# Spreading one zero fill over the DMA engines: six uneven transfers become 28 small ones and a nested tail

## The chip, the cores and the metric

The kernel runs on one core of a Trainium2 chip. The metric is the time of one execution on the device, in microseconds; lower is better. A core has the compute engines TensorE (PE in the profile), VectorE (DVE), ScalarE (ACT) and GpSimd (POOL), SyncE (SP), which here only issues transfers and waits, and 16 DMA engines that move the data.

## The reference

The reference is a decode step of a small transformer block together with its backward pass. Its inputs are one token of width 448, a K cache and a V cache of 8 heads x 32768 positions x 256, and the weights, all bfloat16. Only the last 4096 positions of the caches are read.

```python
h  = x + attention(layernorm(x), K[:, :, -4096:], V[:, :, -4096:], wq, wo)   # 16 query heads, 8 K/V heads
h2 = h + ((layernorm(h) @ w_gate) * (layernorm(h) @ w_up)) @ w_down
out, vjp = jax.vjp(forward, x, K, V, wq, wo, w_gate, w_up, w_down)
return out, *vjp(grad_out)
```

The gradients of K and V have the full shape of the caches, 8 x 32768 x 256 each (134 MB). Only their last 4096 positions of each head are computed; the other 28672 are zero and have to be written all the same. These zeros are most of the bytes that the kernel moves.

## The kernel before, in words

The work has four stages. The first goes over the eight K/V heads `g`: it loads K and V of the window (2 MB each, `load_kv`), computes the scores and the softmax (`scores`) and the sums that the backward pass needs (`moments`). The second does the output projection, the second layernorm and the gated layer, forward and backward. The third (`dq_all`) makes the gradient of the queries. The fourth goes over the heads again, makes the gradients of K and V for the window, and stores them from ScalarE's queue (`LD`, L739, 16 stores of 2 MB), while GpSimd makes the weights' gradients and stores them from its own queue.

Beside all this run the zero fills. There are 16 regions (8 heads, K and V), each of 28672 x 256 elements, 14 MB. The first two (`EARLY`) are written from the tile `pair`, the other 14 by `fill_late` from the tile `home` (`Z_late`), of whose rows every fourth partition, 0, 4, ..., 124, is kept at zero (`clear_rows`). A row is 8192 elements (`ZW`), 16 KB; a region is 896 rows, and a fill is one transfer, 32 partitions x `NZ` = 28 copies. SyncE (`ZQ`) issues the fills one after another: fill `i` waits until fill `i-2` has landed (`DEEP` = 2 semaphores, `zsem`), so that two are under way at any time. All transfers are issued by `fill_with` (L244), whose semaphore goes up by 16 when a transfer has landed. At the end `fills_done` lets VectorE wait for all fills (`psem` for GpSimd's transfers, `zsem` for SyncE's) and write `done_t` (L287).

One fill, that of region 3 (`UNEVEN`, the second of `fill_late`), is not written as one transfer. 22 x 32 of its rows are; the other 192 are written by six transfers of `e` source partitions x `rows` copies each, four from GpSimd's queue (3x8, 2x2, 3x13, 8x13) and two from SyncE's (4x5, 1x1), all ahead of the fill's main part.

The order on each engine is that of the program: `tc.keep_in_program_order` holds the fills and their waits in place, and they are set aside from the scheduler's own dependences. GpSimd's four transfers stand behind its loads of V for heads 5 and 6 (L207) and ahead of its load of the second half of the last K (L418).

Of the kernel before, what the change touches and what calls it, by code (L numbers as in the profile page):

```python
# [27 lines left out]
ZW = 16 * KB  # L28
# [7 lines left out]
def kernel(  # L36
        ctx, tc, A_x, A_k_cache, A_v_cache, A_wq, A_wo, B_x, B_w_gate, B_w_up, B_w_down, grad_out,
           out_0, out_1, out_2, out_3, out_4, out_5, out_6, out_7, out_8):
    nc = tc.nc
    LD = nc.scalar  # L40
    ZQ = nc.sync
# [29 lines left out]
    Z_late = home[:]  # L71
# [134 lines left out]
    def load_kv(dst, cache, g, queue=LD):  # L206
        queue.dma_start(out=dst, in_=cache[0, g, Sk - W:, :].rearrange("(p t) d -> p t d", t=T))  # L207
# [32 lines left out]
    def rows_of(src, n):  # L240
        return src[0:128:4].unsqueeze(1).to_broadcast([32, n, src.shape[1]])

    def fill_with(dst, src, sem, group, queue=ZQ):
        fill = queue.dma_start(out=dst, in_=src)  # L244
        tc.info.no_tile_sem_insts.add(fill.ins.name)
        tc.add_to_no_dep_group(group, fill.ins)
        tc.keep_in_program_order(fill.then_inc(sem, 16))
# [7 lines left out]
    for g in (5, 6):  # L255
        load_kv(V_of[g], A_v_cache, g, nc.gpsimd)

    def fill_late():
        zsem = [tc.alloc_semaphore(f"zsem{j}") for j in range(DEEP)]
        psem = tc.alloc_semaphore("psem")  # L260
        due = [0] * DEEP
        for i, reg in enumerate(regions[EARLY:]):
            j = i % DEEP
            if i >= DEEP:
                tc.keep_in_program_order(ZQ.wait_ge(zsem[j], due[j]))
            n = NZ
            if i + EARLY == UNEVEN:
                odd = reg.rearrange("(r f) -> r f", f=ZW)[22 * 32:]
                reg = reg[0:22 * 32 * ZW]
                n = 22  # L270
                at = 0
                for e, base, rows, queue in ((3, 0, 8, nc.gpsimd), (2, 12, 2, nc.gpsimd), (3, 20, 13, nc.gpsimd), (8, 64, 13, nc.gpsimd), (4, 0, 5, ZQ), (1, 0, 1, ZQ)):
                    fill_with(odd[at:at + e * rows].rearrange("(e n) f -> e n f", e=e),
                              Z_late[base:base + 4 * e:4].unsqueeze(1).to_broadcast([e, rows, ZW]), zsem[j] if queue is ZQ else psem, "fills", queue)
                    at += e * rows
                    if queue is ZQ:
                        due[j] += 16
            for dst, src in [(reg.rearrange("(p n f) -> p n f", p=32, f=ZW), rows_of(Z_late, n))]:
                fill_with(dst, src, zsem[j], "fills")
                due[j] += 16  # L280
        return zsem, psem, due

    def fills_done(zsem, psem, due):
        tc.keep_in_program_order(nc.vector.wait_ge(psem, 64))
        for j in range(DEEP):
            tc.keep_in_program_order(nc.vector.wait_ge(zsem[j], due[j]))
        filled = tc.keep_in_program_order(nc.vector.memset(done_t[:], 0.0))  # L287
        tc.declare_fence(filled.ins, group="fills")
# [43 lines left out]
    with tc.tile_pool(name="ps_x", bufs=1, space=bass.MemoryType.PSUM) as ps_x, \  # L332
# [72 lines left out]
        for g in range(G):  # L405
            p_f = p_next
            if g < G - 2:
                p_next = scores(g + 1)
            if g == 1:
                clear_rows()  # L410
                fill_sems = fill_late()
            moments(g, p_f)
            for w, h in NEXT.get(g, ()):
                load_kv((K_of, V_of)[w][h], (A_k_cache, A_v_cache)[w], h)
            if g == G - 4:
                LD.dma_start(out=K_of[G - 1][:, 0:T // 2, :], in_=k_last[:, 0:T // 2, :])
            if g == G - 2:
                nc.gpsimd.dma_start(out=K_of[G - 1][:, T // 2:, :], in_=k_last[:, T // 2:, :])  # L418
                p_next = scores(G - 1)
                LD.dma_start(out=wo_sb[:, JW:], in_=wo_v[:, JW:])  # L420
                LD.dma_start(out=dh_bc[0:1, :], in_=A_x.rearrange("a b d -> (a b) d"))
# [179 lines left out]
    with tc.tile_pool(name="work2", bufs=2) as work2, tc.tile_pool(name="lnw", bufs=1) as lnw, \  # L601
# [94 lines left out]
        for it, g in enumerate((6, 1, 3, 4, 5, 0, 7, 2)):  # L696
# [52 lines left out]
            if it == 6:  # L749
# [16 lines left out]
                nc.vector.tensor_copy(out=dx_bf[:, 384:D], in_=dx_ps[0:1, 384:D])  # L766
                LD.dma_start(out=out_1.rearrange("a b d -> (a b) d"), in_=dx_bf)
        fills_done(*fill_sems)

# [28 lines left out]
```

## Time and profile before

| what | value |
|---|---|
| median of 3 runs | 779.52 us (779.39 to 779.62) |
| the profiled execution | 779.39 us; span 777.6 us |
| granted clock of TensorE, mean | 0.74 |
| bytes moved | 330.40 MB, 425 GB/s over the span |
| HBM read, written | 49.38 MB, 280.59 MB |
| packets of SyncE's queue, ScalarE's, GpSimd's | 14826, 4266, 4272 |
| last store of a computed gradient issued | 747.9 us of the span |
| last fill issued by SyncE | 661.7 us of the span |

The span runs from the first to the last instruction; the execution's own time is 1.8 us longer. In the profile, the 40 digits of a row show how busy an engine was in each fortieth of the span, in tenths. The row DMA is the mean over the 16 DMA engines. The queue of a transfer is named by the engine that issues it: q1 is SyncE's, q10 ScalarE's and q0 GpSimd's. All three use the same 16 DMA engines. "x" behind a group is its count; a name such as `out_dram<-home` gives what is written and from what.

### The profile page before, as it was taken

The numbers are of one execution on the slowest core, as the hardware profiler recorded it, in microseconds if no ns is written. First come the engines' busy times: TensorE is split into PE (matmuls) and PEld (weight loads), VectorE is DVE, ScalarE is ACT, GpSimd is POOL, SyncE is SP. The second block draws the span as 40 slices with busy tenths as digits, with TensorE's granted clock in tenths as the row PEclk, the third lists the DMA queues.
The fourth block names the chain that finished last, engine by engine and source line by source line (L and its number), as shares of the span: only waits on it lengthen the run. The fifth ranks groups of instructions, "written<-read, shape, count | busy, mean of one in ns | idle before, by whom it ended". The sixth has DMA issues, their size and how long they took to land.

```text
span 777.6 us, 6520 instructions
## 1 busy us (share of the span) xinstructions
PE 450.8 (58%) x2205; PEld 191.2 (25%) x2205; DVE 382.6 (49%) x1132; ACT 198.6 (26%) x309; POOL 196.5 (25%) x113
## 2 busy tenths in 40 slices
PE   1999999796993755231142898532108886830310
PEld 1444444342441322010021233210003332300100
DVE  8168656351570723332369428463104853679520
ACT  1442332334200100000001127332103733540220
POOL 7000001000000010020001157363293938196000
PEclk9999999898896776555555799755558965765555
DMA  9999999999999999999999999999999999999997
GB/s 378 429 422 423 433 438 417 429 429 427 429 430 430 429 430 429 431 431 428 429 432 432 430 429 430 431 429 431 432 432 429 429 429 430 431 429 428 432 431 300
DMA packets 23398, 330.40 MB, mean 425 GB/s; under 512 B 1920, under 2 KB 2181, under 8 KB 4645
## 3 DMA queue, kind: packets, MB, share of 16 engines
q1 hardware_dynamic: 14826, 250.43, 75.4%
q10 hardware_dynamic: 4266, 53.39, 16.1%
q0 software_dynamic: 4272, 26.17, 8.0%
q8 instruction: 17, 0.28, 0.1%
q14 instruction: 17, 0.13, 0.0%
HBM read 49.38 MB, written 280.59 MB: 424 GB/s over the span
## 4 chain that ended last, share of the span: by engine, by line
DVE 16%; PE 15%; DMA 14%; another core or an unknown queue 4%; ACT 2%; issue 1%; DVEq 0%; ACTq 0%
DMA out_dram<-arena 11%; PE d_ps L729 4%; PE rows_ps L322 4%; DVE pair L753 3%; PE tr_ps L319 3%; DVE arena L737 3%; DVE arena L736 3%; DVE arena L551 2%; PE dqb_ps L607 2%; DVE arena L704 1%; DMA arena<-in_B_w_up_dram 1%; PE dqb_ps L613 1%; DMA arena<-in_A_v_cache_dram 1%; ACT arena L734 1%
## 5 line engine op out<-in xcount | busy, mean ns | idle before, releaser
L381 DVE TENSOR_SCALAR arena<-arena,p_f 128x256 bf16<-128x256 bf16 x512 | 109.4, 281 | 29.9 <-PE M_t L385 29.9
L319 PE MATMUL tr_ps<-ident_f,arena 128*128 128x128 f32 x448 | 83.0, 316 | 63.1 <-DMA arena<-in_A_v_cache_dram 41.0
L322 PE MATMUL rows_ps<-arena,vpad 128*16 128x512 bf16 x256 | 87.8, 437 | 11.8 <-DVE arena L704 5.9
L338 ACT COPY arena<-tr_ps 128x1024 bf16<-128x1024 bf16 x64 | 63.5, 1013 | 109.0 <-PE tr_ps L319 105.0
L319 PEld LDWEIGHTS tr_ps<-ident_f,arena 128*128 128x128 f32 x448 | 55.3, 157 | 109.8 <-issue 60.5
L729 PE MATMUL d_ps<-arena 32*128 32x512 bf16 x256 | 48.3, 519 | 55.1 <-DVE arena L737 45.1
L385 PE MATMUL M_t<-arena 128*128 128x512 bf16 x320 | 78.7, 392 | 0.0
L736 DVE CAST arena<-d_ps 128x512 bf16<-128x512 f32 x64 | 44.1, 688 | 49.6 <-PE d_ps L729 48.9
L737 DVE CAST arena<-d_ps 128x512 bf16<-128x512 f32 x64 | 43.5, 680 | 20.9 <-DMA out_dram<-arena 20.9
L733 ACT CAST arena<-d_ps 128x512 bf16<-128x512 f32 x64 | 37.8, 590 | 62.0 <-PE d_ps L729 60.2
L702 ACT COPY arena<-tr_ps 128x1024 bf16<-128x1024 bf16 x32 | 32.6, 1020 | 76.2 <-PE tr_ps L319 57.1
L734 ACT CAST arena<-d_ps 128x512 bf16<-128x512 f32 x64 | 38.2, 596 | 20.5 <-DMA out_dram<-arena 20.5
L385 PEld LDWEIGHTS <-arena 128*128 128x128 bf16 x320 | 30.5, 101 | 38.5 <-issue 10.1
L505 PE MATMUL r_ps<-arena,X2pad 128*2 128x448 bf16 x24 | 10.3, 564 | 49.5 <-DMA arena<-in_B_w_gate_dram 39.1
L324 DVE COPY rows_t<-rows_ps 16x512 f32<-16x512 f32 x8 | 5.4, 679 | 63.4 <-PE rows_ps L322 63.3
L729 PEld LDWEIGHTS <-arena 32*128 32x128 bf16 x256 | 11.1, 96 | 94.1 <-DVE arena L737 60.2
L624 POOL TENSOR_SCALAR arena<-dh_bc,oX_f 128x448 bf16<-128x448 bf16 x18 | 25.1, 1402 | 27.9 <-DMA out_dram<-arena 27.8
L207 POOL DMA_DIRECT2D pair<-in_A_v_cache_dram x2 | 1.3, 632 | 114.7 <-POOLq L253 114.7
L436 POOL DMA_DIRECT2D arena<-in_B_w_gate_dram x4 | 3.1, 773 | 105.9 <-DVE dhn L495 64.5
L704 DVE COPY arena<-tr_ps 128x1024 bf16<-128x1024 bf16 x32 | 22.5, 704 | 14.7 <-PE tr_ps L319 13.4
L322 PEld LDWEIGHTS <-vpad 128*16 128x16 bf16 x256 | 17.4, 90 | 45.0 <-issue 41.0
L385 PE MATMUL M_t<-arena,pair 128*128 128x512 bf16 x128 | 28.0, 379 | 0.0
(257 smaller groups left out, 641.3 us busy)
## 6 DMA issues: line engine op xcount, KB each, us to landing
out_dram<-home SPq DMA_DIRECT2D x13, 14336.0 KB, 78.9
out_dram<-arena ACTq DMA_DIRECT2D x16, 2048.0 KB, 18.6
out_dram<-pair SPq DMA_DIRECT2D x2, 14336.0 KB, 93.6
out_dram<-home SPq DMA_DIRECT2D x1, 11264.0 KB
arena<-in_A_k_cache_dram ACTq DMA_DIRECT2D x4, 2048.0 KB, 20.7
arena<-in_A_k_cache_dram SPq DMA_DIRECT2D x3, 2048.0 KB, 19.6
arena<-in_A_v_cache_dram SPq DMA_DIRECT2D x3, 2048.0 KB
arena<-in_A_v_cache_dram ACTq DMA_DIRECT2D x3, 2048.0 KB, 32.8
```

The source lines that it names most:

```text
L319: nc.tensor.transpose(tr_ps[:, i, :], X_sb[:, 4 * q + i, :].bitcast(f32), ident_f[:])
L322: nc.tensor.matmul(rows_ps[:], lhsT=pad[:, e, 16 * q:16 * q + 16], rhs=XT.rearrange("p (n e) -> p n e", e=2)[:, :, e], start=(q == 0 and e ...
L338: sT_ps = dots(K_of[g], KT_slot, vpad[g % 2], rows1, ps_c, "cols", lambda q, XT, ps: nc.scalar.copy(out=XT, in_=ps))
L381: nc.vector.tensor_scalar(out=pK[:, i, hh, :], in0=K_sb[:, t, :], scalar1=p_f[:, 8 * i + c, hh:hh + 1], scalar2=None, op0=ALU.mult)
L385: nc.tensor.matmul(M_ps[vh], lhsT=V_sb[:, t, vh * 128:(vh + 1) * 128], rhs=pK[:, i, :, :].rearrange("p h d -> p (h d)"), start=(t == 0), s ...
L702: nc.scalar.copy(out=XT, in_=ps)
L704: nc.vector.tensor_copy(out=XT, in_=ps)
L729: nc.tensor.matmul(d_ps[:, qi].rearrange("p w d -> p (w d)"), lhsT=rm[32 * q:32 * (q + 1), l, :], rhs=Rs[32 * q:32 * (q + 1), :], start=Tr ...
L733: nc.scalar.copy(out=stV[:, t:t + 2, :], in_=d_ps[:, :, 0, :])
L734: nc.scalar.copy(out=stK[:, t:t + 2, :], in_=d_ps[:, :, 1, :])
L736: nc.vector.tensor_copy(out=stV[:, t:t + 2, :], in_=d_ps[:, :, 0, :])
L737: nc.vector.tensor_copy(out=stK[:, t:t + 2, :], in_=d_ps[:, :, 1, :])
```

## The change

The uneven fill is spread in another way. Its main part falls from 22 copies of each of the 32 partitions to 14, 448 rows. The other 448 rows go in two sets. GpSimd issues 28 transfers ahead of the main part, in 14 pairs: for `m` from 1 to 14, one of `m` partitions x 1 row and one of `16 - m` partitions x 2 rows. SyncE issues 14 transfers behind the last fill of all, of 14 partitions x 1 row, then 13, and so on down to 1, with no wait between them; they count on the semaphore of the last fill, and the last wait on it grows with them. A new helper, `fill_rows`, writes `k` partitions (0, 8, 16, ... from `8 * e0`) x `n` rows. `psem` is waited for at 28 x 16 instead of 64. The number of bytes is the same, and nothing else is changed.

```diff
+    def fill_rows(rows, at, e0, k, n, sem, queue):
+        fill_with(rows[at:at + k * n].rearrange("(e n) f -> e n f", e=k),
+                  Z_late[8 * e0:8 * (e0 + k):8].unsqueeze(1).to_broadcast([k, n, ZW]), sem, "fills", queue)
+
...
             n = NZ
             if i + EARLY == UNEVEN:
-                odd = reg.rearrange("(r f) -> r f", f=ZW)[22 * 32:]
-                reg = reg[0:22 * 32 * ZW]
-                n = 22
+                n = 14
+                single = reg.rearrange("(r f) -> r f", f=ZW)[n * 32:]
+                reg = reg[0:n * 32 * ZW]
                 at = 0
-                for e, base, rows, queue in ((3, 0, 8, nc.gpsimd), (2, 12, 2, nc.gpsimd), (3, 20, 13, nc.gpsimd), (8, 64, 13, nc.gpsimd), (4, 0, 5, ZQ), (1, 0, 1, ZQ)):
-                    fill_with(odd[at:at + e * rows].rearrange("(e n) f -> e n f", e=e),
-                              Z_late[base:base + 4 * e:4].unsqueeze(1).to_broadcast([e, rows, ZW]), zsem[j] if queue is ZQ else psem, "fills", queue)
-                    at += e * rows
-                    if queue is ZQ:
-                        due[j] += 16
+                for m in range(1, 15):
+                    for e0, k, rows in ((0, m, 1), (m, 16 - m, 2)):
+                        fill_rows(single, at, e0, k, rows, psem, nc.gpsimd)
+                        at += k * rows
             for dst, src in [(reg.rearrange("(p n f) -> p n f", p=32, f=ZW), rows_of(Z_late, n))]:
                 fill_with(dst, src, zsem[j], "fills")
                 due[j] += 16
+        for k in range(14, 0, -1):
+            fill_rows(single, at, 0, k, 1, zsem[j], ZQ)
+            due[j] += 16
+            at += k
         return zsem, psem, due
 
     def fills_done(zsem, psem, due):
-        tc.keep_in_program_order(nc.vector.wait_ge(psem, 64))
+        tc.keep_in_program_order(nc.vector.wait_ge(psem, 28 * 16))
```

In the program as built, the very first of GpSimd's transfers, one partition x one row, is written as 16 pieces of 512 elements; every other one keeps its rows of 8192 elements.

## The prediction

> **What bounds the kernel now.** I read the page first, its slices and queues.
>
> ```profile
> span 777.6 us, 6520 instructions
> PE 450.8 (58%) x2205; PEld 191.2 (25%) x2205; DVE 382.6 (49%) x1132; ACT 198.6 (26%) x309; POOL 196.5 (25%) x113
> ...
> DMA  9999999999999999999999999999999999999997
> ...
> q1 hardware_dynamic: 14826, 250.43, 75.4%
> q10 hardware_dynamic: 4266, 53.39, 16.1%
> q0 software_dynamic: 4272, 26.17, 8.0%
> ```
>
> No compute engine is busy for more than 58%, while the 16 DMA engines are full in every slice but the last; the queue shares add up to 99.6% of their span. q1 is SyncE's queue, q10 ScalarE's, q0 GpSimd's. So the bytes set the time, and the open question is how evenly the 16 engines finish. Next, the timeline and the stretches of the end:
>
> ```profile
> 746.36 1.55 ACTq L739 DMA_DIRECT2D out_dram<-arena  x2
> 776.50 0.06 DVE L287 MEMSET done_t<- 1x1 f32 x1 [29.61 <-DMA out_dram<-home]
> 700.00:747.00 47.00, 8.61 (x48) 3.06 (x48) 35.77 (x41) 9.32 (x17) 13.14 (x3) 0.50 1.01 431
> 747.00:762.00 15.00, 0.00 (x0) 0.00 (x0) 0.00 (x0) 0.00 (x0) 0.00 (x0) 0.50 1.01 433
> ```
>
> After 747.9 us no compute is left; VectorE waits 29.61 us for the fills, and all engines stay full until past 762. Compute has about 19 us of room: from 747 on an engine moves 47 rows (28.9 us at 0.61), of which the last two stores are 16, 9.8 us. Last, the DMA slices of 765 to 777.6 us alone:
>
> ```profile
> DMA  7979798969698969686747221321101010000000
> q1 hardware_dynamic: 126, 1.80, 33.4%
> ```
>
> The share falls from 9 to 0 over some 7 us: the engines run dry one after another, and the last sets the end.
>
> **Which engine is last.** The trace has each DMA packet's queue, start, duration and bytes, but no engine. It can be worked out: a packet starts 3 or 4 ns before the one ahead of it on its engine ends, and each engine must follow the order of rows of each queue. I strung all packets into 16 chains so. A 16 KB row takes 0.611 us, so 0.607 net. The chains show where the uneven fill's 192 rows go: GpSimd's four transfers lie on engines 0-2 (8 rows each), 3-4 (2), 5-7 (13) and 8-15 (13), next to one another; SyncE's on 0-3 (5 each) and on 0 (1). An engine with no part in a GpSimd transfer gets a 4-byte packet per row instead: 13x8 + 14x2 + 13x13 + 8x13 = 405, just what q0 has beyond its 37x16 completions. I number the engines by these places. Sums: engine 0 has 14 rows, 1 and 2 have 13, 3 has 7, 4 has 2, the rest 13. The ends, us of the span:
>
> ```
> engine 0: 770.4; 1 and 2: 770.9, 771.5; 3: 774.1; 4: 775.9
> engines 5-15: 769.2 769.4 769.6 772.1 772.2 772.2 772.4 772.4 772.4 772.6 774.4
> ```
>
> Mean 772.0. So engine 4, with the fewest rows, is still last. Its packets run over: between 42 and 748 us most of its rows take 3 to 60 ns (a few up to 140) too long, 13.4 us in all, where most engines lose 1 to 2. (Engines 4 to 15 have equal histories after the uneven fill, so chains can change places where two end together; I read the overrun, which leaves one chain and begins in another at 315.8 and at 550.0 us, as one engine.) Engine 3 carries most of the 8 KB packets of q14, 0.31 us each and some 0.35 more for the row behind.
>
> **The change part by part.** The uneven fill's plain part falls from 44 rows an engine to 28: -16 on all. The 14 nested SyncE transfers put 14 rows on engine 0 down to 1 on 13, none on 14 and 15 (before: 4 rows wide on engines 0-3, 1 wide on 0; lowest first). So engine 4 gains 10 there. GpSimd's 28 transfers are pairs of m engines x 1 row and 16-m x 2 rows; if each starts where the last ended, as the four of before did, engine e should get 14+e (14 and 15: 28), and all reach 28. But in the built program the first, a single row, is cut in 16 pieces of 1 KB; it would lie on all engines and move the start by none, so all later ones slip one engine down: engine 15 gets 13, the others 14+e+1 (14: 28). That slip I take as likeliest, since a whole turn of 16 leaves the place as it was. Engine 4: 19 + 10 - 2 - 16 = +11 rows (as described: +10). Engine 3: +6, 0: -1, 15: -16, others 0 or -1.
>
> Sum on engine 4: 11 x 0.607 = 6.68; its usual overrun, 13.4 us over 1,458 packets, 9 ns a row: 0.10; 22 more 4-byte packets (60 for 38) at 9-4 = 5 ns: 0.11; the 1 KB piece 0.04 (896 B took 41 ns). Together 6.9 us. Engine 3 ends at 774.1 + 3.6 = 777.7, so engine 4's 775.9 + 6.9 = 782.8 decides. What lies behind its last packet (landing 0.4, the wait, the memset, 1.1 to the span's end) stays. The profiled execution took 779.39, 1.8 more than its span; the median is 779.52. 779.39 + 6.9 = 786.3.
>
> GpSimd's issues: 28 at 0.61 (four took 2.44) are 17 us from 131.4 on, against 2.4.
>
> ```profile
> 131.40 2.44 POOL L244 DMA_DIRECT2D out_dram<-home  x4
> 235.18 0.57 POOL L418 DMA_DIRECT2D arena<-in_A_k_cache_dram  x1 [101.34 <-PE ok_ps L390]
> ```
>
> The next, L418, waits 101 us for PE, which hides them; were that gone, 15 us of delay would still fit compute's 19. But L418's packets queue in q0 behind the rows. A q0 entry waits a turn of SyncE's row: 70 entries (28 rows at most, 42 small ones) from about 164 us, where the two loads ahead land, take 28 x 1.22 + 42 x 0.62 = 60 us, and some 7 of ScalarE's loads: to 231. L418 at 235 is just clear; 10 us of delay would also hide. The 28-row part between two fills is the thinnest place in SyncE's queue: fill 0 lands over 9 us (185.4 to 194.4), 28 rows beside q0 last 34, so no engine runs dry.
>
> SyncE's own queue is blocked when its rows stand deep:
>
> ```profile
> 71.09 49.23 SPq L244 DMA_DIRECT2D out_dram<-home  x3
> ```
>
> Issue times inside are 38.3, 8.0 and 2.9 us (a fill's usual one: 0.53). The 8.0 ends when 132.7 of q1's packets per engine are gone and 196 were issued with the fill ahead: 64 left. So I take it that some 64 packets per engine stand in line and the rest waits. The tail is issued behind the last fill (661.7), is let in from about 716, and needs 28 places on engine 0, one row time each (0.6 to 1.2 us): done by 750, with over 40 rows standing. Nothing waits behind it on SyncE but the end. Bounds: none, or 14 x 8.0 = 112 us from 716; I take none, since the 8.0 was a wait for room, and rooms open while the rows run.
>
> The many small transfers as such: their rows took 0.611 us before, as those of 14 MB fills, and full queues hide each landing, so nothing is added. [...]
>
> **Rivals.** (1) *Each GpSimd transfer of single rows starts at engine 0 and does not move the start.* Then pairs pile up low: the two-row ones (119 places in turn) give engine 4 16 rows, the single ones 10, the tail 10: +18 rows, 10.9 + 0.3 us: 790.6. For it: no transfer of before has this shape (row by row, no repeat). Against: the four did move on. [...] (2) *The tail enters late:* 8 us each while rows stand, then one row at a time: by 776 some 8 of 14 are in, 6 more at 0.6 to 2.5 us: +4 to +15 on 786.3, so 790 to 801. (3) *The change does as described*, 28 each: +10 rows, 785.7. (4) *Not slower:* the overrun does not stay with one engine; the two breaks, at 315.8 and 550.0 us, are real, and the chain that ends at 775.9 is one of 5 to 15, the chain of engine 4 one that ends at 769.6. Place: engine 4's chain; price: its 6.9 us fall into room that is there, 769.6 + 6.9 = 776.5, or 775.9 as described, beside a last end of 775.9 that gains nothing or loses up to 16 rows. With engine 3's 774.1 then also another's (its place among 1 to 3 rests on the same reading), the time is 778.0 to 780.0. For it: the identities rest on the overrun's going over from row to row. It decides if engine 4 ended before 770.6.
>
> **How the numbers follow.** Slip 0.48, as described 0.16, rival 1 0.19, rival 2 0.07, rival 4 0.10 (0.03 of it faster by over 0.2%). Predicted: 786.3. Range 785.2 to 791.0 holds the first three, 0.83, with 0.5 us at both ends for small terms. A measurement here tells 0.2%, 1.6 us, from no change: faster 0.03, same 0.07, slower 0.90.
>
> **Right or wrong.** Right: the fills' last landing trails the others by some 5 us on one engine, the DMA share of the last 12 us falls slowly with a long tail, q1 has 448 + 14 nested rows, VectorE's last wait grows by 7 us, compute ends near 747. The chains should show engine 15 with 13 rows of GpSimd. Wrong: a last landing by engine 3 or 0, SyncE issues after 760, or an end with all engines within 3 us.

## The result, and the profile after

The changed kernel takes 818.69 us (median of 4, 816.45 to 819.63) against 779.52 before: ratio 1.0498, 95% interval 1.0474 to 1.0523. The forecast was 786.3, range 785.2 to 791.0. The sign was right; the loss is 39.2 us where 6.8 were expected.

The page of the changed kernel, in the order in which I read that of before:

```profile
span 817.9 us, 6538 instructions
...
DMA  9999999999999999999999999999999999999971
GB/s 381 428 417 427 430 430 427 428 346 337 321 372 423 426 425 431 431 430 427 430 433 430 430 432 429 429 431 429 433 419 429 429 426 428 428 432 429 342 299 55
...
q1 hardware_dynamic: 14754, 247.61, 72.4%
q10 hardware_dynamic: 4266, 53.39, 15.3%
q0 software_dynamic: 4752, 28.99, 9.5%
```

The row DMA says "full" to the last slices, just as before. The row GB/s below it does not: slices 9 to 12 (164 to 245 us) fall to 321 to 372, and the last three to 342, 299 and 55. The engines are busy and move less. The same in stretches of the changed kernel (time, busy us of PE, PEld, DVE, ACT, POOL, clock, DMA share, GB/s):

```profile
160.00:245.00 85.00, 65.94 (x377) 29.97 (x381) 36.84 (x171) 21.35 (x30) 0.55 (x1) 0.90 1.01 347
245.00:290.00 45.00, 19.12 (x71) 9.17 (x73) 12.27 (x56) 4.50 (x8) 0.00 (x0) 0.62 1.01 426
290.00:750.00 460.00, 213.71 (x945) 86.67 (x943) 224.05 (x485) 111.57 (x181) 179.09 (x97) 0.66 1.01 429
750.00:775.00 25.00, 8.57 (x48) 3.02 (x48) 13.83 (x27) 9.31 (x17) 0.00 (x0) 0.50 0.93 367
775.00:795.00 20.00, 0.00 (x0) 0.00 (x0) 0.00 (x0) 0.00 (x0) 0.00 (x0) 0.50 0.81 315
795.00:817.90 22.90, 0.00 (x0) 0.00 (x0) 0.06 (x1) 0.00 (x0) 0.00 (x0) 0.50 0.18 69
```

and of the kernel before, for the first of them:

```profile
160.00:245.00 85.00, 66.75 (x382) 29.98 (x381) 36.84 (x171) 21.36 (x30) 0.57 (x1) 0.91 1.01 429
```

A share of 1.01 at 347 GB/s instead of 429 means that packets take longer. So I counted them: after 150 us, 23 of the 16 KB rows took over 0.7 us before, 529 in the changed kernel, up to 4.0 us, 340 us too long in all. Of these, 370 lie between 160 and 256 us, while GpSimd's small transfers are under way, and 92 from 764 us on, while SyncE's nested ones are. Most of the others stand in short bursts of q1 rows near 603, 632 and 675 us, which no run here explains. The slow rows are not only the small transfers' own: 170 are of q0, 346 of q1, where the plain fills run beside.

The end, by the timeline of the changed kernel, and the DMA slices of its last 12 us:

```profile
774.13 4.38 ACTq L745 DMA_DIRECT2D out_dram<-arena  x2
816.74 0.06 DVE L293 MEMSET done_t<- 1x1 f32 x1 [42.09 <-DMA out_dram<-home]
```

```profile
DMA  2020302200220022000500022002200010000000
DMA packets 38, 0.31 MB, mean 26 GB/s; under 512 B 19, under 2 KB 19, under 8 KB 19
```

VectorE still waits for the fills last. Compute ends 28 us later than before, under the cover of the fills. The last 12 us are two engines running alone. Up to 807.2 us one of them still has rows of the plain fill, and the rows of both take 0.611 us. From 808 us on both are in their nested rows, and each row takes 1.273 us while both run; the last one, alone, takes 0.622. In this last stretch the two together move what one engine moves elsewhere (16 KB in 0.611 us, 27 GB/s).

GpSimd's issues are as forecast, SyncE's end some 10 us later than that:

```profile
131.58 15.20 POOL L244 DMA_DIRECT2D out_dram<-home  x28
242.71 0.55 POOL L424 DMA_DIRECT2D arena<-in_A_k_cache_dram  x1 [95.92 <-PE ok_ps L396]
```

```profile
682.69 78.25 SPq L244 DMA_DIRECT2D out_dram<-home  x15
```

28 issues took 15.2 us, and GpSimd still waits 95.92 us for PE behind them; the last fill and the tail behind it were all issued by 761.

### The profile page after: what moved, and what is told of

It reads as the page before. It is cut to its first block, busy times and chain, and to the rows that moved or that the text cites. A ratio compares the mean times of both kernels' runs of the same rounds, so it can differ in the third digit from the quotient of the medians.

```text
span 817.9 us, 6538 instructions
## 1 busy us (share of the span) xinstructions
PE 444.4 (54%) x2187; PEld 190.2 (23%) x2205; DVE 383.6 (47%) x1132; ACT 198.6 (24%) x309; POOL 210.9 (26%) x137
## 4 chain that ended last, share of the span: by engine, by line
DVE 15%; DMA 14%; PE 13%; another core or an unknown queue 5%; ACT 2%; issue 1%; DVEq 0%; ACTq 0%
DMA out_dram<-arena 11%; PE d_ps L735 3%; PE rows_ps L328 3%; DVE pair L759 3%; DVE arena L743 3%; DVE arena L742 3%; PE tr_ps L325 2%; DVE arena L557 2%; PE dqb_ps L613 2%; DMA arena<-in_B_w_up_dram 1%; DVE arena L710 1%; DMA arena<-in_A_v_cache_dram 1%; PE dqb_ps L619 1%; ACT arena L740 1%
## 5 line engine op out<-in xcount | busy, mean ns | idle before, releaser
L325 PE MATMUL tr_ps<-ident_f,arena 128*128 128x128 f32 x448 | 81.3, 311 | 89.7 <-DMA arena<-in_A_v_cache_dram 48.5
L328 PE MATMUL rows_ps<-arena,vpad 128*16 128x512 bf16 x256 | 85.8, 429 | 12.5 <-DVE arena L710 5.8
L630 POOL TENSOR_SCALAR arena<-arena,xT 128x4096 bf16<-128x4096 bf16 x2 | 21.2, 10617 | 26.3 <-DMA out_dram<-arena 26.3
```

The source lines that it names most:

```text
L325: nc.tensor.transpose(tr_ps[:, i, :], X_sb[:, 4 * q + i, :].bitcast(f32), ident_f[:])
L328: nc.tensor.matmul(rows_ps[:], lhsT=pad[:, e, 16 * q:16 * q + 16], rhs=XT.rearrange("p (n e) -> p n e", e=2)[:, :, e], start=(q == 0 and e ...
L630: nc.gpsimd.tensor_scalar(out=buf[:, off:off + n], in0=src, scalar1=col, scalar2=None, op0=ALU.mult)
```

## The experiments

Three theories of the slow rows. **S**: the source partitions. Before, the small transfers read partitions 4 apart (`base + 4 * e`); the change reads them 8 apart. **D**: the destination, neighbouring rows written by one transfer. **N**: the mere number of small transfers. Every ratio is against the kernel before on the same chip.

**src8**: the kernel before, with its small transfers reading 8 apart.

```diff
-  (3, 0, 8, gpsimd), (2, 12, 2, gpsimd), (3, 20, 13, gpsimd), (8, 64, 13, gpsimd), (4, 0, 5, ZQ), (1, 0, 1, ZQ)
-  Z_late[base:base + 4 * e:4]
+  (3, 0, 8, gpsimd), (2, 24, 2, gpsimd), (3, 40, 13, gpsimd), (8, 64, 13, gpsimd), (4, 0, 5, ZQ), (1, 0, 1, ZQ)
+  Z_late[base:base + 8 * e:8]
```

> The kernel before, with one thing of the change: its six small transfers read partitions 8 apart (0, 8, 16 / 24, 32 / 40, 48, 56 / 64 to 120; 0, 8, 16, 24 / 0) instead of 4 apart. Rows, engines, destinations and queues are as before. In the changed kernel 529 rows took over 0.7 us (0.611 is usual), 340 us too long in all, and nearly all of them while its 448 small-transfer rows were moving: 0.76 us for each such row. Theory S (source): the rows are slow because of the partitions that they are read from. Then 192 rows x 0.76 = 146 us over 16 engines, 9 us on the mean engine and some 13 on the worst: 786 to 793 us, with rows over 0.7 us between 164 and 200 us of the span. Theory D (destination: neighbouring 16 KB rows of the output written at the same time) and theory N (many small transfers as such): 779.5 us, no slow rows.

Measured 792.71 us, ratio 1.0163 (1.0148 to 1.0178), with 211 rows over 0.7 us and the same dip, by the stretch of src8:

```profile
160.00:245.00 85.00, 60.61 (x317) 26.73 (x316) 31.72 (x148) 21.46 (x30) 0.00 (x0) 0.80 1.01 397
```

But the end is another one, as the timeline of src8 shows:

```profile
776.07 0.94 ACTq L739 DMA_DIRECT2D out_dram<-arena  x2
780.77 0.06 DVE L287 MEMSET done_t<- 1x1 f32 x1 [4.18 <-DMA out_dram<-home]
```

The fills end only 4.3 us later than before (780.77 for 776.50). The last stores were issued 30 us later and set the span (790.8): PE waited 36.4 us instead of 19.6 for K between 160 and 330 us; I read this as loads that stand in line behind slow rows. So theory S holds for the rows, while most of this kernel's loss came through compute, whose room the slow rows used up.

**dst1**: the kernel before, each small transfer writing interleaved rows.

```diff
-  odd[at:at + e * rows].rearrange("(e n) f -> e n f", e=e)
+  odd[at:at + e * rows].rearrange("(n e) f -> e n f", e=e)
```

> The kernel before, with its six small transfers writing their rows interleaved, so that the engines of a transfer write neighbouring rows of 16 KB at the same time, as in the changed kernel; sources, counts and engines as before. Theory D: slow rows as in the changed kernel, 786 to 793 us. Theories S and N: 779.5 us and rows of 0.611 us.

Measured 779.36, ratio 0.9998 (0.9989 to 1.0008); 22 slow rows. D falls.

**even8** and **even_own**: the change with even `m` alone and twice the copies (14 GpSimd transfers and 7 nested ones, none of single rows; 28 rows for each engine), once with sources 8 apart, once with 4 apart from 32 on. Partitions 4e and 32 + 4e for engine e of 0 to 7, 32 + 4e for 8 to 15, are called the engine's own place here: small rows read there left 23 slow rows in before and 21 in even_own. That an engine reads the same place in a plain fill is inferred from this; no trace names a packet's partition.

```diff
-  for m in range(1, 15):  ((0, m, 1), (m, 16 - m, 2))        ...  for k in range(14, 0, -1):  k x 1 row
+  for m in range(2, 15, 2):  ((0, m, 2), (m, 16 - m, 4))     ...  for k in range(14, 0, -2):  k x 2 rows
   Z_late[8 * e0:8 * (e0 + k):8]                 # even8
   Z_late[32 + 4 * e0:32 + 4 * (e0 + k):4]       # even_own
```

> The changed kernel with every small transfer doubled in rows and halved in number: GpSimd's pairs are m x 2 rows and (16-m) x 4 rows for even m (14 transfers), the tail 14, 12, ..., 2 partitions x 2 rows (7 transfers). Still 28 of the 448 rows for every engine, but no transfer is of single rows, so by the rule seen in the kernel before each starts where the last ended and none piles up on the low engines. Sources 8 apart as in the change. Count alone (engine 4 +10 rows of 0.607): 785.6 us. Theory S: the same number of rows from the same partitions, so the same 340 us too long, 21 on the mean engine and up to 29 on the worst: 803 to 815 us. Theory N: half as many transfers, half the loss: about 797. Theory D: as S.

> As even8, but the small transfers read partitions 4 apart from 32 on (engine e reads partition 32 + 4e). Theory S: no slow rows, and the count alone remains: engine 4, last before, has 10 rows more: 779.4 + 6.1 + 0.1 = 785.6 us (785 to 786.5). Theory D: as even8, 803 to 815. Theory N: about 797.

even8: 811.57, ratio 1.0419 (1.0401 to 1.0436), 442 slow rows. even_own: 785.75, ratio 1.008 (1.0065 to 1.0095), 21 slow rows. One slice apart, 25.8 us. The stretch of each, even8's first:

```profile
160.00:245.00 85.00, 61.36 (x336) 27.90 (x336) 36.84 (x171) 20.35 (x29) 0.00 (x0) 0.86 0.96 348
```

```profile
160.00:245.00 85.00, 66.47 (x385) 30.05 (x383) 36.85 (x171) 21.36 (x30) 0.56 (x1) 0.92 1.01 429
```

N falls too: 15 more small transfers than before cost nothing that the row count doesn't explain. even_own's chains can be strung to the end: engine 4 ends at 782.2, engine 3 at 776.9, the rest by 774. That is the prediction's own arithmetic, 28 each, 10 rows more on engine 4: 785.7.

**even_next**: even_own with every source moved to the partition that the next engine reads.

```diff
-  Z_late[32 + 4 * e0:32 + 4 * (e0 + k):4]
+  Z_late[36 + 4 * e0:36 + 4 * (e0 + k):4]
```

> even_own (785.75) with one thing changed: each engine's small rows are read from the partition beside its own (36 + 4e for engine e, in place of 32 + 4e), so 15 different places for 16 engines, where even8's partitions 8 apart were 8 different places. S1 (what costs is that a row is read through another engine's place, whoever else reads there): 798 to 812 us, with 250 or more rows of over 0.7 us after 150 us, nearly as even8 (811.57; 442 such rows). S2 (what costs is that two small rows meet at one place, which partitions 8 apart force by leaving 8 places): 785.7 to 788 us, under 60 such rows.

Measured 807.63, ratio 1.0353 (1.0334 to 1.0372), 485 slow rows. S1: sources at 36 + 4e in place of 32 + 4e make 485 slow rows, against 21. That 8 apart leaves 8 places, as S2 puts it, is an estimate: the runs show two such pairs, 0 and 32 (pair_meet) and 16 and 48 (the changed kernel's end), both at 1.273 us a row. I read S1 so: the loss needs no two small rows at one place; it is enough that the row is read where another engine, by the inference above, reads its fills. Yet its last sixteen rows, on one engine alone, took 0.611 us but for one. So a foreign place is not slow by itself, which the runs of pairs below take up.

**even_tail8**: even_own with the nested tail alone 8 apart.

```diff
-  fill_rows(single, at, 0, k, 2, zsem[j], ZQ)          # from 32, 4 apart
+  fill_rows(single, at, 0, k, 2, zsem[j], ZQ, 0, 8)    # from 0, 8 apart
```

> even_own (785.75) with the nested SyncE tail alone read from partitions 8 apart; GpSimd's rows stay on their own. even8 against even_own is 25.8 us for both parts. If the slow rows cost in proportion to their number (112 tail rows of 448, GpSimd's 336 the rest): 785.8 + 25.8 x 112 / 448 = 792.2, range 789 to 796. If the tail costs more for its number, since its rows stand at the end on the few engines that finish last and nothing evens out behind them: 796 to 806. If the tail does not count: 785.8 to 787.

Measured 796.37, ratio 1.0217 (1.0204 to 1.0231): 10.6 us over even_own, at the lower edge of the second case. 112 rows of 448, a quarter, make 41% of the 25.8 us; I put that down to the engines that end last, on which they fall with nothing behind them to even out.

**even_single**: where single-row transfers lie, with every source in its own place if rival 1 is right.

```diff
-  for m in range(2, 15, 2):  ((0, m, 2), (m, 16 - m, 4))
+  for m, e0, k in ((2, 0, 14), (14, 14, 2), (4, 0, 12), (12, 12, 4), (6, 0, 10), (10, 10, 6), (8, 0, 8)):
+      ((0, m, 1), (0, m, 1), (e0, k, 4))
```

> Where single-row transfers of GpSimd lie, alone: even_own (785.75) with each of its seven 2-row transfers split in two single-row ones, and the 4-row ones in an order that never wraps from engine 15 to 0 if the single ones do not move the start; each row is read from the engine's own partition if that holds. Single-row ones on engines 0 to m-1, start not moved (rival 1's rule): engine totals of the fill 72 on 0 and 1, 68, 68, 64, 64 and so on to 40; engine 4 with 18 rows more than before (46) ends at 775.9 + 18 x 0.607 + 0.3 = 787.1, so 779.5 + 11.2 = 790.7, range 789.5 to 792, under 60 rows of over 0.7 us. Single-row ones that move the start as the others do: engine 4's total is 58 in place of 64, and most rows miss their engine's place: 795 to 815, with 200 or more slow rows.

Measured 790.91, ratio 1.0146 (1.0129 to 1.0163), 20 slow rows: rival 1's rule. By the prediction's rule most rows would have missed their place, and there would be hundreds.

**after_own2**: the changed kernel's transfers as they are, sources aimed at the engines' own places.

```diff
+  OWN = [0, 32, 28, 20, 72, 56, 36, 76, 80, 48, 76, 36, 56, 72, 84]
-  for e0, k, rows in ((0, m, 1), (m, 16 - m, 2)):                           # from 8 * e0, 8 apart
+  for base, k, rows in ((48 if m == 8 else 32, m, 1), (OWN[m], 16 - m, 2)):  # from base, 4 apart
```

> The changed kernel's 28 + 14 transfers as they are, with the same destinations, and only the source partitions changed: each row is read from the reading engine's own place, as far as one slice can say it, by the placement read from the changed kernel's chains (single-row transfers of m engines on engines 0 to m-1 without moving the start, the 8-wide one excepted; the two-row ones from the moving start; some 40 of 448 rows still miss their engine's place where a two-row transfer wraps from engine 15 to 0). Placement as read, engine 4 with +16 rows: 779.5 + 16 x 0.607 + 0.3 = 789.5, up to 793 with the 40 rows that miss. The prediction's slip (engine 4 +11): the sources then miss too, but with the placement of the slip the chains would show engine 15 with 13 rows of GpSimd; time 786.3 and above. If the slow rows of the changed kernel had nothing to do with the source: 815 to 820.

Measured 794.60, ratio 1.0194 (1.0181 to 1.0207), above my range: 279 slow rows, more than 40 misses explain, 229 of them between 160 and 235 us, in GpSimd's part. Its packets can be strung up to 199 us. They place the transfers by rival 1's rule as far as they go: the first row in 1 KB pieces on all engines, the single rows of 2 to 5 engines on 0 up, the two-row ones starting at 0, 15, 13, 10. What I had wrong was the order within a transfer that goes from engine 15 on to 0. The one from 13 by way of 15 to 9 has slow rows (0.8 to 2.4 us) on engines 0 to 2 and 6 to 9, and none on 13 to 15, where my sources missed. That fits a first share on the lowest number, not on the start; then every row of such a transfer missed. It is inferred from this one transfer, and no other run shows it. The exception that I made for the 8-wide single rows was wrong too: even_single has two such, read from engine 0's place on, and no more slow rows than before. So the run bounds what the change costs with better sources, but doesn't isolate the placement; even_single does.

**pair_own, pair_next, pair_meet**: two engines alone at the end, differing only in where they read.

```diff
-  main part 22 x 32 rows
+  main part 20 x 32 rows, and behind the last fill one SyncE transfer of 2 partitions x 32 rows from
+  Z_late[0:8:4]       # pair_own:  engine 0 reads its own place, engine 1 its own
+  Z_late[4:12:4]      # pair_next: engine 0 reads that of 1, engine 1 that of 2
+  Z_late[0:64:32]     # pair_meet: both read that of 0
```

> The kernel before with 64 of the uneven fill's rows moved from its plain part (44 rows an engine down to 40) to one more SyncE transfer behind the last fill: 32 rows on engines 0 and 1 each, read from partitions 0 and 4, which are these engines' own. Engines 0 and 1 get 28 rows more, 17.0 us, and run alone at the end: 771.5 + 17.0 = 788.5 in place of 775.9, so 779.5 + 12.6 = 792.1 by every theory, and the last rows take 0.611 us each.

> pair_own with the 64 rows read from partitions 4 and 8, each the place of the engine beside, which has no rows left soon after. M (a place gives its rate to one engine, and two that read there at once share it): the last rows take 0.611 us, time 792 to 795. F (a row read through another engine's place is slow by itself): the last rows of both engines take about 1.27 us, as the changed kernel's last ones did: 769 + 32 x 1.27 = 809.7, so 811 to 814.

> pair_own with the 64 rows read from partitions 0 and 32, both the place of engine 0. M: both engines' last rows take 1.27 us while both run, 769 + 32 x 1.27 = 809.7, time 811 to 814. F: engine 0's rows take 0.611 us and end with the others, engine 1's 1.27 us to the end: also 811 to 814, but then the rows of the end are of two lengths, 0.611 beside 1.27 until 788, and one engine alone at 1.27 behind it. If neither matters with so few engines running: 792.

Measured (two executions of each) 791.84, 794.08 and 811.02; ratios 1.0156 (1.0127 to 1.0186), 1.0185 (1.0155 to 1.0214), 1.0402 (1.0372 to 1.0432). A stretch of the end in which two engines run, of pair_own, pair_next and pair_meet in turn:

```profile
775.00:787.00 12.00, 0.00 (x0) 0.00 (x0) 0.00 (x0) 0.00 (x0) 0.00 (x0) 0.50 0.13 55
```

```profile
775.00:787.00 12.00, 0.00 (x0) 0.00 (x0) 0.00 (x0) 0.00 (x0) 0.00 (x0) 0.50 0.12 52
```

```profile
775.00:790.00 15.00, 0.00 (x0) 0.00 (x0) 0.00 (x0) 0.00 (x0) 0.00 (x0) 0.50 0.13 26
790.00:805.00 15.00, 0.00 (x0) 0.00 (x0) 0.00 (x0) 0.00 (x0) 0.00 (x0) 0.50 0.12 25
```

The share is the same, 2 of 16 engines; the rate is 55, 52 and 26 GB/s. In pair_meet every row between 776 and 804 us takes 1.273 us, on both engines, and the last one, alone, 0.611: M, not F. The nine slow rows at pair_next's end all lie before 776 us, while the neighbours still run. The 1.273 us are also those of the changed kernel's rows from 808 us on, and its last 12 us move 26 GB/s in the mean.

**tuned**: the kernel before, with engine 4 relieved by 6 rows, every source in its own place and no single rows.

```diff
-  main part 22 x 32;  (3, 0, 8, gpsimd), (2, 12, 2, gpsimd), (3, 20, 13, gpsimd), (8, 64, 13, gpsimd), (4, 0, 5, ZQ), (1, 0, 1, ZQ)
+  main part 19 x 32;  (3, 0, 12, gpsimd), (2, 12, 2, gpsimd), (3, 20, 20, gpsimd), (2, 64, 18, gpsimd), (6, 72, 20, gpsimd), (4, 0, 8, ZQ)
```

> The kernel before, with the uneven fill's plain part at 38 rows an engine in place of 44 and 288 small rows in six transfers, all read from the engine's own partition, every small transfer of several rows: against before engine 4 has 6 rows less, 3 has 3 less, 8 and 9 one less, 0 to 2 and 5 to 7 and 10 to 15 one more. Ends by the chains of before and even_own: engine 4 775.9 - 3.6 = 772.3, 3 772.3, 8 or 9 773.8 (by even_own, which has the same one row less there), the others up to 773.2. So the last end goes from 775.9 to 773.8: 777.3 us, ratio 0.997; range 776.3 to 779.0. If the last end does not follow engine 4's rows (another engine is held up in its place, or the compute chain): 779.0 to 781.

Measured 778.40 (776.92 to 781.47, 12 runs), ratio 0.9988 (0.9980 to 0.9997). Its median is 1.1 us below that of before, about half of what I expected, and the interval only just excludes no change. In its profile VectorE's memset behind the fills stands at 775.40, 1.1 us earlier than before. Its runs spread over 4.6 us, where those of before beside it spread over 1.0; I have not found why, and which engine ends last in the slower ones stays open.

## Why the prediction was right or wrong

- **What sets the time: right.** The packets of 16 engines, and the engine that ends last. even_own (785.75 for 785.7), even_single (790.91 for 790.7) and pair_own (791.84 for 792.1) came out of engine ends of before plus rows x 0.607 us.
- **"Their rows took 0.611 us before … so nothing is added": wrong, the step that failed.** I priced a small transfer's row by the rows of before without asking what made those cheap: each engine read its small rows at its own place (23 slow rows in before). The change's slice, 8 apart, sends engines to others' places (529 slow rows), and two that read at one place at once take 1.273 us for a row (pair_meet). The plain fills beside them lose about as much: between 150 and 256 us q0's slow rows are 137 us too long, q1's 122. With the placement of rival 1 and every source in its own place the kernel would take 790.6 (even_single, with the same 18 rows more on engine 4, took 790.91); the other 28.1 us are this (a remainder; even8 against even_own, as many rows otherwise placed, has 25.8). Rows of up to 4.0 us stand only where all engines run; that these are the same sharing among more readers is argued, not shown. The size of the transfers was not it: even_single, with two of 32 KB and 28 small transfers in all, took the time of its rows (790.91 for 790.7), with 20 slow ones.
- **The slip, taken as likeliest: wrong.** Its first half is right: the first row was cut in 1 KB pieces on all engines and moved the start by none. But the other single-row transfers don't move it either; they start at engine 0. That is rival 1's rule (0.19). In the changed kernel the chains show it up to about 184 us, for the single rows of 2 engines and the 14-wide transfer behind them, which starts at 15; even_single shows the time. It makes +18 rows on engine 4, +11 us.
- **No engine runs dry, GpSimd's issues are hidden: right.** The share stays at 1.01 to 750 us.
- **Compute ends near 747: wrong.** Its last stores were issued at 774 to 778. PE's wait for K between 160 and 330 us is 38.2 us, 18.6 more. L424 was issued at 242.71, 7.5 later, and would have hidden; I put the rest down to the slow rows ahead of the loads. It costs the changed kernel nothing, because the fills end at 816, but in src8 it set the end.
- **The tail is let in early (rival 2 falls): right.** In from 733.6 after a wait of 50.4 us, the last issue from 759.7 to 760.9, against "from about 716, done by 750" and 760 as a sign against it; the shift is no more than the last fill's own, 682.7 for 661.7. No run shows the 2.5 us that rival 2's sum sets as the most for a late transfer; behind that wait the other 13 issues took 27.3 us, 2.1 us each.
- **Rival 4 (in the kernel before, another engine than 4 is the last): refuted** by even_own, whose engine 4 ends 6.2 us later for 10 rows.
- **The last landing on one engine, engine 4: wrong.** Two engines run to the end, and neither is 4. The tail puts 14 - e rows on engine e: in after_own2 the chains of the end have 14, 13 and so on down to 0 rows behind the last fill's. In the changed kernel the two last chains, strung from the end, have 8 and 12 such rows, so they are engines 6 and 2, which read partitions 48 and 16, both the place of engine 4. They end at 816.3 and 815.5 us of the span; the chain with 10, engine 4, ends at 803.4. By rival 1's count engine 6 has only three rows more than before (1.8 us), so nearly all of its delay is something other than the number of its rows.

So 779.5 + 11.1 (placement) + 28.1 (shared places) = 818.7. The two terms split the time, not the work of one engine: 11.1 is what engine 4 would add if every row took 0.611 us, and 28.1 is what is left.

## What to carry to other kernels

When rows are spread by hand over DMA engines, choose the source partition together with the engine: here each engine had to read at its own place (even_own 785.75 us; even_next, one place on, 807.63), and two engines at one place at the same time took 1.273 us for a row in place of 0.611. A row of full DMA shares does not show the loss (1.01 at 347 GB/s as at 429); hold it against the GB/s below it, and look at the durations of packets. A transfer of the same queue but another shape (here one row per partition, without a repeat) is another case: its placement needs a run of its own, as even_single was (790.91 us, where the moving start was expected to give 795 to 815).

## What the runs showed of the hardware

- Two engines that read at one place at once take 1.273 us for a 16 KB row, 2.08 times the 0.611 us of one alone (pair_meet, and the end of the changed kernel); a foreign place that nobody else uses leaves a row at 0.611 (pair_next, from 776 us on).
- GpSimd's single-row transfers of 2 to 5 partitions start at engine 0 and leave the start of the next as it was (after_own2's chains; the two-row ones between start at 0, 15, 13, 10), whereas those of several rows go on from where the last ended (even_own's chains: engine 4 ends at 782.2, as 28 rows for each engine give).
- One engine of the 16, engine 4, ends last in before (13.4 us of overrun in the whole kernel), even_own and after_own2; in the latter two the last chain has ten rows behind the last fill's, as engine 4 must. Why it runs over stays open.
